# Re-ordering the start-up of a fused linear-attention and token/channel-mixer kernel on one core

## The chip, the cores and the metric

The kernel runs on one core of a Trainium2 chip. The metric is the device time of one execution in microseconds (us). All times come from the hardware profiler or from timed runs on a chip.

## The reference

For each of 8 batches (8 heads, 576 rows, head size 64): linear attention with the feature map phi, then token mixing over the 576 rows, then channel mixing over the 512 columns, both with a residual.

```python
def phi(x):
    return np.where(x > 0, x, np.exp(x) - 1.0) + 1.0
q_p, k_p = (phi(q), phi(k))
kv = np.einsum('bhsd,bhse->bhde', k_p, v)
z = np.sum(k_p, axis=2)
num = np.einsum('bhsd,bhde->bhse', q_p, kv)
den = np.einsum('bhsd,bhd->bhs', q_p, z)[..., None] + 1e-06
x = num / den                                    # then heads are joined: (8, 576, 512)
# ...
h = np.maximum(x.T @ w_tok1, 0.0) @ w_tok2       # per batch, over the rows
u = x + h.T
out = u + np.maximum(u @ w_ch1, 0.0) @ w_ch2     # 512 -> 1536 -> 512
```

## The kernel before

The instructions of each engine stand in the order in which the program emits them. TensorE does every product. ScalarE does exp, relu, the casts of v and most copies out of PSUM (the banks in which TensorE leaves its products). VectorE does the rest of phi, the division and the residual adds. SyncE issues the loads of q, k, v and the output stores; GpSimd issues the weight loads. A batch passes through these helpers:

```python
def phi(nm, n, h0, nh):          # exp on ScalarE, then add, min, max on VectorE
    # ...
    nc.scalar.activation(out=e, in_=f, func=AF.Exp)
    nc.vector.tensor_scalar(out=y, in0=f, scalar1=1.0, scalar2=None, op0=ALU.add)
    nc.vector.tensor_scalar(out=e, in0=e, scalar1=1.0, scalar2=None, op0=ALU.min)
    nc.vector.tensor_tensor(out=dst[...], in0=e, in1=y, op=ALU.max)
# vcast: v to bf16 on ScalarE; kv: k^T v; qtr: transposes of q; nd: numerator and denominator,
# then den + EPS, reciprocal and multiply on VectorE; mm1, mm2: token mixing; utr: transposes of u;
# mm3: first channel product; mm4: second channel product, then:
    o = outp.tile([128, DM], FP32, name="o_sb", tag="o_sb")      # outp has 3 buffers
    nc.vector.tensor_tensor(out=o, in0=ps, in1=u[b][:, r, :], op=ALU.add)
    nc.sync.dma_start(out=..., in_=o)
```

Batch 0 is emitted in its natural order. The preparation of batch 1 is then laid between the 24 steps ("slots") of batch 0's channel mixing, 12 of mm3 and 12 of mm4; in each of the latter, four sums of output rows grow by one weight block.

```python
c_in = [load_wc1(i) for i in range(NB)]
for g in range(2):
    landed["k1", g] = load("k", 1, g, c_in[1] if g == 0 else None)
for g in range(2):
    landed["v1", g] = load("v", 1, g)
c2_in = [after(load_wc2(0), landed["k1", 1])]
# ...
warm(40)                         # dummy matmuls
prep_k(0, 0)                     # phi of k, cast of v, for the first four heads
kv(0, 0)
warm(16)
phi("q", 0, 0, 2)
phi("q", 0, 2, 2)
qtr(0, 0)
prep_k(0, 1)
# ...
kv(0, 1)
for h0 in (4, 6):
    phi("q", 0, h0, 2)
qtr(0, 1, split=True)
# ... nd, mm1, mm2, utr, the first part of mm3
for nm in "kvq":
    for g in range(2):
        load(nm, 2, g, c2_in[2] if nm == "k" and g == 0 else None)   # batch 2, behind w_ch2
# ...
at0 = {"kv0": 13, "kv1": 15, "qt0": 19, "qt1": 21, "nd00": 22, "nd01": 22, "nd10": 22,
       "nd11": 22, "nd20": 23, "nd21": 23, "mm1": 23, "mm2a": 23, "mm2b": 23, "mm2t": 23,
       "ut": 23, "utt": 23}
fill += [(s, lambda g=g: prep_k(1, g)) for g, s in ((0, 11), (1, 12))]
fill += [(s, lambda g=g: prep_q(1, g)) for g, s in ((0, 17), (1, 19))]
```

## Time and profile before

| | before |
|---|---|
| median of the first 3 runs (range) | 317.94 us (315.82 to 318.87) |
| profiled span, granted clock of TensorE | 313.3 us, 0.953 |
| first matmuls of nd (numerator and denominator) | 16.60 us |
| second part of batch 0's channel matmuls | 42.51 us |
| batch 1's mm1 (first token matmuls) | 76.26 us |
| batch 1's channel matmuls | 86.47 us |

The profiled execution took 315.84 us, which is near the kernel's fastest.

The head of the page gives each engine's busy time, its share of the span and its instructions:

```profile
span 313.3 us, 4856 instructions
...
PE 276.7 (88%) x1882; PEld 153.6 (49%) x1882; DVE 168.4 (54%) x331; ACT 167.9 (54%) x257; POOL 10.6 (3%) x20
```

TensorE (PE) works 277 us, so nearly all that can be won is the 37 us in which it stands still. How to read the other views: a slice row gives one digit for each fortieth of the span, in tenths busy. A timeline line reads start, length, engine, line of the program, operation, output<-inputs, shape, count, and in square brackets how long the engine had been idle before it and what released it. A matmul is called hot or cold by whether its run of like matmuls takes the shorter or the longer of the two times that the traces show for it. A window line reads start:end, length, then busy time and count of PE, PEld, DVE, ACT and POOL, the granted clock, the mean busy share of the DMA engines, and GB/s.

### The profile page before, as it was taken

How to read it: one execution, taken by the hardware profiler on the slowest of the kernel's cores; microseconds unless marked ns; L12 is line 12 of the kernel's file. 1: busy time of each engine (PE TensorE's matmuls, PEld its weight loads, DVE VectorE, ACT ScalarE, POOL GpSimd, SP SyncE). 2: the span in 40 equal slices, each digit the busy share in tenths (PEclk: the TensorE clock that was granted, in tenths of full speed). 3: DMA queues.
4: the chain of work that ended last, by engine and by line, in shares of the span. 5: the costliest groups of instructions: out<-in, count | busy, mean ns of one | idle time of the engine just before them, and what ended most of it. 6: DMA issues, size and time to landing. Idle time of an engine off the chain costs nothing.

```text
span 313.3 us, 4856 instructions
## 1 busy us (share of the span) xinstructions
PE 276.7 (88%) x1882; PEld 153.6 (49%) x1882; DVE 168.4 (54%) x331; ACT 167.9 (54%) x257; POOL 10.6 (3%) x20
## 2 busy tenths in 40 slices
PE   4646689873798998999999999999999999999994
PEld 4534333441345544655566546545656455454641
DVE  6554340665447479487737760879276816250021
ACT  2552247830289835874688726765877447225600
POOL 2330300000000000000000000000000000000000
PEclk9575999996999999999999999999999999999998
DMA  7999999604979349509721972001000130011022
GB/s 209 275 168 267 280 188 271 186 0 159 294 195 304 109 150 280 174 4 273 246 69 48 273 234 70 0 33 69 35 2 1 69 100 2 18 49 70 0 67 100
DMA packets 47958, 41.82 MB, mean 133 GB/s; under 512 B 14656, under 2 KB 43200, under 8 KB 47936
## 3 DMA queue, kind: packets, MB, share of 16 engines
q1 hardware_dynamic: 43648, 37.76, 41.5%
q0 software_dynamic: 4288, 3.77, 7.7%
q8 instruction: 14, 0.23, 0.3%
q14 instruction: 8, 0.07, 0.1%
HBM read 35.85 MB, written 9.44 MB: 145 GB/s over the span
## 4 chain that ended last, share of the span: by engine, by line
PE 74%; DVE 9%; ACT 8%; DMA 4%; issue 3%; SPq 0%; ACTq 0%; DVEq 0%
PE h_ps L274 26%; PE c_ps L251 24%; PE a_ps L195 6%; PE h_ps L209 4%; ACT e L117 4%; PE kv_ps L138 3%; PE tp L152 3%; PE nd_ps L170 3%; PE c_ps L262 3%; PE tp L227 2%; DVE x L178 2%; DVE u L216 2%; DMA q_raw<-in_q_dram 2%; DMA k_raw<-in_k_dram 1%; DVE o_sb L280 1%
## 5 line engine op out<-in xcount | busy, mean ns | idle before, releaser
L251 PE MATMUL c_ps<-uT,wc 128*128 128x512 bf16 x384 | 92.6, 379 | 3.5 <-ACT cr L255 1.5
L274 PE MATMUL h_ps<-wc,cr 128*128 128x512 bf16 x384 | 90.0, 379 | 0.0
L255 ACT ACTIVATE cr<-c_ps 128x512 bf16<-128x512 f32 x96 | 56.9, 598 | 51.3 <-PE c_ps L251 51.1
L274 PEld LDWEIGHTS <-cr 128*128 128x128 bf16 x384 | 36.7, 98 | 40.6 <-issue 0.3
L251 PEld LDWEIGHTS <-wc 128*128 128x128 bf16 x384 | 35.4, 98 | 36.6 <-issue 4.3
L119 DVE TENSOR_SCALAR e<-e 128x1280 bf16<-128x1280 bf16 (+1 forms) x34 | 16.0, 471 | 39.6 <-ACT e L117 39.6
L280 DVE TENSOR_TENSOR o_sb<-h_ps,u 128x512 f32<-128x512 f32 x32 | 21.8, 685 | 22.3 <-PE h_ps L274 20.0
L178 DVE TENSOR_TENSOR x<-nd_ps,den 128x512 bf16<-128x512 f32 (+1 forms) x48 | 28.9, 602 | 1.7
L175 DVE TENSOR_SCALAR den<-nd_ps 128x8 f32<-128x8 f32 (+1 forms) x48 | 7.7, 161 | 36.5 <-PE nd_ps L170 36.0
L216 DVE TENSOR_TENSOR u<-h_ps,x 128x1024 bf16<-128x1024 f32 (+1 forms) x18 | 19.2, 1098 | 11.4 <-PE h_ps L209 11.4
L170 PE MATMUL nd_ps<-kvbd,qT 128*128 128x130 bf16 x160 | 18.3, 230 | 6.2 <-DVE x L178 4.1
L195 PE MATMUL a_ps<-x,w 128*128 128x512 bf16 (+1 forms) x72 | 19.0, 394 | 5.2 <-DVE den L175 5.2
L231 ACT COPY uT<-tp 128x1024 bf16<-128x1024 bf16 x8 | 8.1, 1012 | 28.5 <-PE tp L227 28.5
L198 ACT ACTIVATE ar<-a_ps 128x512 bf16<-128x512 f32 (+1 forms) x18 | 8.9, 545 | 27.0 <-PE a_ps L195 27.0
L170 PEld LDWEIGHTS <-qT 128*128 128x128 bf16 x160 | 12.7, 102 | 17.7 <-DVE x L178 6.0
L161 ACT COPY qT<-tp 128x1280 bf16<-128x1280 bf16 x15 | 18.5, 1231 | 4.5 <-PE tp L152 4.5
L117 ACT ACTIVATE e<-k_raw 128x1280 bf16<-128x1280 f32 x16 | 20.3, 1269 | 0.1
L117 ACT ACTIVATE e<-q_raw 128x1280 bf16<-128x1280 f32 (+1 forms) x18 | 20.2, 1148 | 0.1
L138 PE MATMUL kv_ps<-vs,kp 128*128 128x130 bf16 x160 | 12.8, 231 | 6.9 <-DVE kp L120 5.9
L209 PE MATMUL h_ps<-ar,w 128*128 128x512 bf16 (+1 forms) x72 | 16.8, 355 | 1.9 <-ACT ar L198 1.5
L128 ACT CAST vs<-v_raw 128x1024 bf16<-128x1024 f32 x16 | 16.9, 1054 | 0.0
L152 PE MATMUL tp<-identity,qp 128*128 128x128 bf16 x160 | 13.0, 230 | 4.0 <-DVE qp L120 4.0
(54 smaller groups left out, 245.3 us busy)
## 6 DMA issues: line engine op xcount, KB each, us to landing
k_raw<-in_k_dram SPq DMA_DIRECT2D x16, 512.0 KB, 5.1
v_raw<-in_v_dram SPq DMA_DIRECT2D x16, 512.0 KB, 6.2
q_raw<-in_q_dram SPq DMA_DIRECT2D x16, 512.0 KB, 6.0
out_dram<-o_sb SPq DMA_DIRECT2D x32, 256.0 KB, 2.4
wc<-in_moe_w_ch_dram POOLq DMA_DIRECT2D x8, 384.0 KB, 9.8
k_raw<-in_k_dram SPq DMA_DIRECT2D x16, 64.0 KB, 5.0
v_raw<-in_v_dram SPq DMA_DIRECT2D x16, 64.0 KB, 5.9
q_raw<-in_q_dram SPq DMA_DIRECT2D x16, 64.0 KB, 5.8
```

What stands on the lines that cost most here:

```text
L117: nc.scalar.activation(out=e, in_=f, func=AF.Exp)
L138: nc.tensor.matmul(out=ps[:, i, 0:2 * D1], lhsT=kp[b][:, r, 2 * j:2 * j + 2, :], rhs=vs[b][:, r, 2 * j:2 * j + 2, :], start=(r == 0), stop ...
L152: nc.tensor.transpose(out=tp[:, i * R1 + r, :], in_=qp[b][:, r, 2 * j:2 * j + 2, :].rearrange("p a b -> p (a b)"), identity=identity)
L170: nc.tensor.matmul(out=ps[:, i, a * 2 * D1:(a + 1) * 2 * D1], lhsT=qT[b][:, j, r, :], rhs=kvbd[b][:, j, :], start=True, stop=True)
L178: nc.vector.tensor_tensor(out=x[b][:, rs[0]:rs[0] + m, HG * D * g:HG * D * (g + 1)].rearrange("p r (h d) -> p r h d", h=HG), in0=v_[:, :, ...
L195: nc.tensor.matmul(out=ps[:, mt], lhsT=w1t[:, b, ms] if r == R else w1[:, r, ms], rhs=x[b][:, r, cs], start=(r == 0), stop=(r == R))
L209: nc.tensor.matmul(out=ps[:, i], lhsT=w2t[:, kt, b, :] if r == R else w2v[:, kt, r], rhs=ar[b][:, kt, cs], start=(kt == 0), stop=(kt == NT ...
L216: nc.vector.tensor_tensor(out=u[b][:, rs[0]:rs[0] + m, cs], in0=ps[:, 0:m], in1=x[b][:, rs[0]:rs[0] + m, cs], op=ALU.add)
L251: nc.tensor.matmul(out=ps, lhsT=wc1[:, kj, 128 * mc:128 * mc + 128], rhs=uT[b][:, kj].rearrange("p r c -> p (r c)"), start=(kj == 0), stop ...
L255: nc.scalar.activation(out=cr[b][:, mc, :], in_=ps, func=AF.Relu)
L274: nc.tensor.matmul(out=ps, lhsT=crt[:, kc, :] if t == 8 else cr[b][:, kc, 128 * r:128 * r + 128], rhs=wc2[:, kc, :], start=(kc == 0), stop ...
L280: nc.vector.tensor_tensor(out=o, in0=ps, in1=ut[p % 2] if t == 8 else u[b][:, r, :], op=ALU.add)
```

## The change

The intent is to let TensorE begin its dense work sooner, by these parts:

1. Each engine's list for batch 0 is re-ordered by when its data lands: q is loaded ahead of v; the exp table is loaded by a dummy exp during the first load; q's exps of the second half stand ahead of the copies of kv; q is transposed in pairs; the v casts go to GpSimd.
2. 130 dummy matmuls, and some smaller groups, fill the load wait, so that TensorE's clock is up when work comes.
3. Half of batch 0's residual is added by a matmul with the identity, and copied out by ScalarE, beside the other half on VectorE.
4. Batch 1's preparation moves to earlier slots.
5. w_ch2's first quarter is loaded behind batch 1's v instead of its k.
6. Its second quarter is gated on batch 1's q, where it had no gate of its own.

Smaller edits, not in the list or the cut below: w1 is gated on batch 0's q rather than its k, batch 2 is loaded in the order k, q, v, some memsets move to GpSimd, and parts of batch 0 use other PSUM banks.

```diff
-    for nm in "kvq":
+    for nm in "kqv":                       # order of batch 0's loads
+    one = work.tile([128, 1], FP32, name="one", tag="one", bufs=1)
+    nc.vector.memset(one, 0.0)
+    nc.scalar.activation(out=one, in_=one, func=AF.Exp)
 ...
-    warm(40)
-    prep_k(0, 0)
-    kv(0, 0)
+    phi("k", 0, 0, HG)
+    warm(130)
+    phi_exp("q", 0, 0, 2)
+    phi_add("q", 0, 0, HG)
+    phi_exp("q", 0, 2, 2)
+    vcast(0, 0, nc.gpsimd)
+    for j in range(2):
+        phi_end("q", 0, 2 * j, 2)
+        qtr_pair(0, j, bank16(), True)
 ...
+    phi_exp("q", 0, 4, 2)
+    phi_add("q", 0, 4, HG)
+    phi_exp("q", 0, 6, 2)
+    vcast(0, 1, nc.gpsimd)
 ...
+    kv(0, 1, True)
 ...
+    mm2_first(0, [0, 1], True)             # True: residual by an identity matmul
+    mm2_first(0, [2, 3], False)
 ...
-    c2_in = [after(load_wc2(0), landed["k1", 1])]
+    c2_in = [after(load_wc2(0), landed["v1", 0])]
 ...
-    c2_in += [load_wc2(i) for i in range(1, NB)]
+    c2_in += [after(load_wc2(i), landed["q1", 0] if i == 1 else None) for i in range(1, NB)]
 ...
-    at0 = {"kv0": 13, "kv1": 15, "qt0": 19, "qt1": 21, "nd00": 22, "nd01": 22, "nd10": 22,
-           "nd11": 22, "nd20": 23, "nd21": 23, "mm1": 23, ...
+    at0 = {"kv0": 12, "kv1": 12, "qt0": 14, "qt1": 16, "nd00": 17, "nd01": 18, "nd10": 19,
+           "nd11": 20, "nd20": 21, "nd21": 22, "mm1": 23, ...
-    fill += [(s, lambda g=g: prep_k(1, g)) for g, s in ((0, 11), (1, 12))]
-    fill += [(s, lambda g=g: prep_q(1, g)) for g, s in ((0, 17), (1, 19))]
+    fill += [(8, lambda: phi("k", 1, 0, HG)), (9, lambda: phi("k", 1, HG, HG)),
+             (11, lambda: vcast(1, 0)), (12, lambda: vcast(1, 1)),
+             (14, lambda: phi("q", 1, 0, HG)), (14, lambda: phi("q", 1, HG, HG))]
```

## The prediction

> **What bounds it now.** I read the page's forty slices first, then a table of busy time by stretch, then the timeline.
>
> ```profile
> PE   4646689873798998999999999999999999999994
> ...
> PEclk9575999996999999999999999999999999999998
> DMA  7999999604979349509721972001000130011022
> ```
>
> A slice is 7.8 us. TensorE is 90% busy or more nearly everywhere from slice 11 on; the first ten slices are not, and the granted clock dips there to half. So the kernel is bound by TensorE, behind a start-up bound by something else. The stretch table (length, busy us and count of each engine, clock, DMA) sizes both:
>
> ```profile
> 16.60:28.40 11.80, 5.18 (x42) 3.88 (x43) 6.85 (x18) 4.95 (x8) 1.95 (x3) 0.64 1.21 209
> ...
> 66.05:76.26 10.21, 2.88 (x25) 1.50 (x24) 7.17 (x20) 0.57 (x1) 0.00 (x0) 0.82 0.22 79
> 76.26:86.47 10.21, 7.93 (x41) 3.68 (x42) 4.22 (x7) 2.10 (x3) 0.00 (x0) 0.85 1.00 276
> 86.47:140.00 53.53, 50.73 (x370) 28.09 (x368) 35.19 (x72) 39.57 (x60) 0.00 (x0) 1.00 0.61 176
> 140.00:313.30 173.30, 169.24 (x1135) 91.56 (x1132) 89.83 (x166) 93.37 (x143) 0.00 (x0) 0.99 0.27 83
> ```
>
> From 86.47 us, where batch 1's first channel matmuls start, TensorE is busy for 220 of 227 us: nothing to win there, and this part only moves. Everything that the change can gain lies before it. The timeline gives three facts:
>
> ```profile
> 5.73 1.28 ACT L117 ACT_TABLE_LOAD   x1 [5.73 <-DMA k_raw<-in_k_dram]
> ...
> 10.36 0.49 DVE L118 TENSOR_SCALAR y<-q_raw 128x640 bf16<-128x640 f32 x1 [0.68 <-DMA q_raw<-in_q_dram]
> ...
> 42.51 1.46 PE L251 MATMUL c_ps<-uT,wc 128*128 128x512 bf16 x6 [0.78 <-DVE uT L233]
> ...
> 71.34 4.49 SPq L283 DMA_DIRECT2D out_dram<-o_sb  x4
> 74.77 0.69 DVE L280 TENSOR_TENSOR o_sb<-h_ps,u 128x512 f32<-128x512 f32 x1 [2.27 <-DMA out_dram<-o_sb]
> ...
> 76.26 1.89 PE L195 MATMUL a_ps<-x,w 128*128 128x512 bf16 x4 [5.20 <-DVE den L175]
> ```
>
> The table load sits between k's landing and its exp. Batch 0's dependent chain (attention, token mixing, transposes) reaches the second part of its channel matmuls only at 42.51. And the fourth output add waits on VectorE for a free buffer while batch 1's last normalisations stand behind it; TensorE idles 5.20 us and then runs cold.
>
> **What the Trainium skill says.** "ScalarE: Activation LUTs", What ACT_TABLE_LOAD costs: about 1283 ns for the load. The trace agrees: 1.28 us. "TensorE: Matmul & The Clock Gate", Part 1: an idle window of about 3.4 us halves the clock, sustained work restores it. The trace agrees in kind: after the 5.20 us gap the ten matmuls of L195 take 3.85 us, at 112.57 us the same ten take 2.17. "GPSIMD Engine Reference", Engine selection and Specifications: one-input work is roughly line-rate there, and it contends with VectorE for SBUF. The trace before has no such cast; a POOL memset of 512 elements takes 0.52 us. "DMA: Bandwidth & Descriptors", Issuing engines are not separate DMA queues: all queues share the 16 engines. The DMA row agrees: near full until slice 6 whichever queue feeds it.
>
> **Part 1, batch 0's first half.** k lands 5.6 us in. With the table already loaded, exp (1.27) ends at 7.0 rather than 8.29, min (0.49) and max (0.83) at 8.4 rather than 9.68. q is now second, and something second (v) had landed by 8.20 before; two exps of 0.68 end by 9.5, VectorE's add 0.83 and twice min and max (0.32 + 0.49) by 11.0, transposes and two copies of 0.69 by 12.2. v, now third, lands at 10.36; the POOL cast is my estimate, 1.04 us by the memset's rate plus some waiting, so 11.8. Then the kv matmuls (0.57 hot) and two copies (0.54): the nd matmuls start at 13.0 rather than 16.60. That is 3.6 us. The 130 dummies: 40 took 3.79 us before, the last ones about 50 ns each, so 130 end at 9.7 to 11, as q's first pair becomes ready; they cost nothing and keep the clock up.
>
> **Part 2, the second half.** k lands at 12.54, exp now runs 13.0 to 14.3 (16.44 to 17.71 before). VectorE does one normalisation (0.17 + 0.20 + 0.69), then k's min and max, to 15.9. q's exps no longer stand behind the kv copies on ScalarE (they were at 23.18); they end by 16.6, q is ready at 18.4 (26.09 before), qT at 19.5 (28.1 before): 8.6 us. The token matmuls then wait for weights: w1t, issued after the second cast at about 17.6 and 3.5 us to landing, is there at 21; the first half of mm1 ends at 22 (1.1), relu 0.6, and mm2 waits for w2 (issued by 18.8, 4.3 to 5.0 to landing) until 24. The residual by identity moves one of two 0.68 us adds from VectorE to a 0.6 us copy on ScalarE, at two more matmuls, so the halves run side by side: u 25.7, mm1's second half and transposes 26.9, uT 27.6, first channel matmuls (1.46) 29.1, second half of mm2 30.3, u 31.0, transposes and split copies 32. Against 42.51 that is 10.5. I take off 2 by judgement, 1.5 for the shared SBUF port and late weights and 0.5 for cold matmuls: **8.5 us**, start at 34.
>
> **Part 3, batch 1's preparation.** The rest of the channel matmuls takes 9.7 as before (42.51 to 52.20): to 43.7. From 52.20 to 76.26 were 24.06 us: 48 matmuls of h_ps (10.4), 2 kv (1.5), 2 transposes (1.5), 6 nd (2.2) make 15.6, so 8.5 idle. Afterwards the nd steps end a slot before the output adds, which removes the 5.20; their 0.2 to 0.7 us waits, 2.1 in all, spread into slots of matmuls. But the two exps now stand in slots 8 and 9, ahead of the last relus that free the four PSUM banks: 2 us; the vs casts hold up kv by about 1.2, q's chain the transposes by 1.5, others 0.8. So 5.5 idle in place of 8.5: **3 us**.
>
> **Part 4, token stage of batch 1.** mm1 runs hot, 3.85 to 2.16: 1.7. The buffer wait now falls while mm1 runs; only some 0.9 of it comes back in front of the u adds. **0.8 us** net.
>
> **Part 5, the loads.** w1 is gated on q rather than k, and POOL casts v before it issues w1t, w2, wc1: wc1's second quarter lands at some 26 rather than 24.34, and batch 1's loads, gated on it, start 2 us later. k1 then lands near 35, wanted at 39; v1 at 40, wanted at 44; q1 at 43, wanted at 48; w_ch2's quarters from 41 to 48, wanted from 43 on, a quarter each 3 to 4 us. Hidden, with 2 to 5 us to spare.
>
> Sum: 8.5 + 3 + 0.8 = 12.3, and behind it the stream of 227 us unchanged. From the median 317.94: 305.6, call it **305.5 us**.
>
> **Rivals.** First, POOL: if a cast takes 3 us rather than 1.2 (contention, or a slow first call), w1t, w2 and wc1 issue 3 or more later, and mm2 waits for w2; for it speaks that nothing in the trace sizes the cast, against it POOL's memset rate. That gives 309. Second, the transfers replace the waits: the DMA row is full until 46 us, so a shorter compute chain meets k1, v1, q1 and w_ch2 unlanded; about half of the gain is handed back, 311. Against it: before, batch 1's k had landed at 33.17 and was first used at 52.90. Third, the dummies block real work: TensorE works in order, and 130 at the mean of the first 40 (95 ns) would end at 13.7, delaying the first half by 3, the sum by perhaps 2: 307. Fourth, everything goes as worked out and no allowance is needed: 302.
>
> **Range and chances.** The losses are independent and small, the gain sits in one serial stretch that nothing later can take back, since TensorE is full behind it. I take 300 to 311. Faster by 2% means under 311.6, which the three worse rivals only just meet one at a time: 0.92 faster, 0.07 same, 0.01 slower.
>
> **What would show it.** In the trace after: the first nd matmuls at about 13 us; the second part of the channel matmuls at 32 to 36; batch 1's mm1 (ten matmuls of 512) at about 64.5 and in 2.2 us, without the 5 us gap; batch 1's channel matmuls at 74 in place of 86.47; from there to the end 227 us. I am wrong if a POOL cast lasts over 2.5 us, if TensorE waits on a wc or k_raw DMA before 60 us, or if the stretch behind grows, by a load or output store that comes at a worse time.

## The result

| | before | after |
|---|---|---|
| median (range), 4 runs each | 318.18 us (315.82 to 318.87) | 301.06 us (300.62 to 302.12) |
| ratio of the rounds (95%) | 1 | 0.9479 (0.9423 to 0.9536) |
| profiled span, granted clock | 313.3 us, 0.953 | 300.3 us, 0.988 |

A ratio is the mean time of one kernel's runs over the mean of the other's in the same rounds, so it is not quite the ratio of the medians. Executions over 1.5% slower than the fastest of the same kernel are left out of the means. The kernel is faster by 5%, at the lower end of the range given. The profiled pair shows only 13.0 us of the 17 us between the medians: the profile of before is of one of its fastest executions, and that of after is of its slowest (302.12 us). Over the 25 later runs the kernel before spread from 313.82 to 319.67 us. What causes that spread was not found.

The page of the kernel after, with the rows that answer to those of before:

```profile
span 300.3 us, 5077 instructions
...
PE 277.8 (92%) x1992; PEld 158.5 (53%) x1992; DVE 166.9 (56%) x324; ACT 167.4 (56%) x258; POOL 14.0 (5%) x24
...
PE   8968867976899989999999999999999999999994
...
PEclk9989999997999999999999999999999999999999
DMA  7969999997997595097308650011000210011022
```

TensorE's busy time has hardly moved, though 13.5 us of it are now dummies (7.8 before). A slice is 7.5 us, and from slice 10 on none but the last is below 80%. The DMA row is the one to look at: counted from slice 0, it is near full in most slices up to slice 9, 75 us, where before it broke off in slices 7 to 9. The windows of the three late stages:

```profile
42.70:61.36 18.66, 14.28 (x110) 8.10 (x109) 12.38 (x28) 10.58 (x15) 2.45 (x3) 1.00 0.98 208
61.36:72.40 11.04, 6.93 (x41) 3.76 (x40) 5.95 (x9) 2.10 (x3) 0.00 (x0) 0.94 0.83 250
72.40:300.30 227.90, 221.01 (x1502) 119.92 (x1500) 125.20 (x237) 132.89 (x202) 0.00 (x0) 0.99 0.38 113
```

The first is the stage from the last of batch 0's first channel products to batch 1's mm1. It takes 18.66 us, where it took 24.06 before, and the DMA engines are 98% busy in it (44% before). The second, batch 1's token stage, takes 11.04 us for 10.21: it is no shorter. From the timeline of the kernel after, the lines that answer to the prediction's:

```profile
0.75 1.28 ACT L391 ACT_TABLE_LOAD   x1 [0.75 <-PEq L591]
...
9.73 1.05 POOL L146 CAST vs<-v_raw 128x1024 bf16<-128x1024 f32 x1 [6.57 <-DMA v_raw<-in_v_dram]
...
13.63 0.62 PE L196 MATMUL nd_ps<-kvbd,qT 128*128 128x130 bf16 x8 [0.18 <-ACT kvbd L169]
...
32.60 1.70 PE L332 MATMUL c_ps<-uT,wc 128*128 128x512 bf16 x6 [0.67 <-ACT uT L313]
...
38.51 0.74 POOL L417 DMA_DIRECT2D wc<-in_moe_w_ch_dram  x1 [16.13 <-DMA v_raw<-in_v_dram]
...
42.56 2.59 POOL L417 DMA_DIRECT2D wc<-in_moe_w_ch_dram  x3 [3.31 <-DMA q_raw<-in_q_dram]
...
45.43 1.04 PE L355 MATMUL h_ps<-wc,cr 128*128 128x512 bf16 x4 [2.72 <-DMA wc<-in_moe_w_ch_dram]
...
60.32 0.93 SPq L105 DMA_DIRECT2D v_raw<-in_v_dram  x1
...
61.36 1.03 PE L231 MATMUL a_ps<-x,w 128*128 128x512 bf16 x4
...
62.15 6.20 SPq L364 DMA_DIRECT2D out_dram<-o_sb  x4
...
67.31 0.69 DVE L361 TENSOR_TENSOR o_sb<-h_ps,u 128x512 f32<-128x512 f32 x1 [3.98 <-DMA out_dram<-o_sb]
...
69.18 0.59 PE L242 MATMUL h_ps<-ar,w2t 128*128 128x512 bf16 x2 [2.65 <-DVE u L248]
```

The table load is out of the way, nd comes 3.0 us sooner, the second part of the channel matmuls 9.9 us sooner, and mm1 follows without the 5.20 us gap. But two waits are new. At 42.7 us TensorE stands still for 2.72 us, for w_ch2's first quarter, which was issued at 38.51. And the fourth output add waits 3.98 us on VectorE for a store: the stores were issued from 62.15 on, right behind the last load of batch 2 at 60.32 in the same queue. The residual adds of batch 1 stand behind that add, so TensorE waits 2.65 us for them.

In the profiled pair the difference therefore adds up as follows. The channel matmuls of batch 0 start 9.9 us sooner; their second part takes 10.10 us for 9.69, which costs 0.4; the stage up to mm1 gives 5.4; the token stage costs 0.8; the rest of the program takes 227.9 us for 226.8, which costs 1.1. That is 13.0 us. The split is that of one execution. In the profile of after_again, the same kernel run once more (below), the stage up to mm1 takes 20.35 us and gives only 3.7, the token stage takes 9.07 us and gives 1.1, and the rest takes 226.7; the two stages together give 4.6 us in after and 4.9 in after_again.

### The profile page after: what moved, and what is told of

The parts are those of the page before. It is cut to its first block, busy times and chain, and to the rows that moved or that the text cites. A ratio compares the mean times of both kernels' runs of the same rounds, so it can differ in the third digit from the quotient of the medians.

```text
span 300.3 us, 5077 instructions
## 1 busy us (share of the span) xinstructions
PE 277.8 (92%) x1992; PEld 158.5 (53%) x1992; DVE 166.9 (56%) x324; ACT 167.4 (56%) x258; POOL 14.0 (5%) x24
## 4 chain that ended last, share of the span: by engine, by line
PE 70%; DMA 9%; ACT 7%; SPq 5%; DVE 3%; issue 2%; POOL 1%; ACTq 0%; DVEq 0%
PE h_ps L355 28%; PE c_ps L332 23%; PE a_ps L231 4%; PE h_ps L242 4%; SPq L105 3%; PE nd_ps L196 3%; PE c_ps L343 3%; DMA wc<-in_moe_w_ch_dram 3%; DMA v_raw<-in_v_dram 2%; PE tp L175 2%; ACT e L114 2%; PE tp L259 2%; SPq L103 2%; DMA q_raw<-in_q_dram 2%; PE kv_ps L165 2%
## 5 line engine op out<-in xcount | busy, mean ns | idle before, releaser
L332 PE MATMUL c_ps<-uT,wc 128*128 128x512 bf16 x384 | 93.8, 382 | 3.2 <-ACT cr L336 1.5
L128 DVE TENSOR_SCALAR e<-e 128x1280 bf16<-128x1280 bf16 (+1 forms) x34 | 17.0, 500 | 32.9 <-ACT e L114 32.9
L187 ACT COPY qT<-tp 128x1280 bf16<-128x1280 bf16 x14 | 17.2, 1231 | 2.1 <-PE tp L175 2.1
L248 DVE TENSOR_TENSOR u<-h_ps,x 128x1024 bf16<-128x1024 f32 x14 | 16.5, 1217 | 0.7 <-PE h_ps L242 0.7
L234 ACT ACTIVATE ar<-a_ps 128x512 bf16<-128x512 f32 x14 | 7.5, 592 | 15.7 <-PE a_ps L231 15.7
L242 PE MATMUL h_ps<-ar,w 128*128 128x512 bf16 x56 | 14.4, 379 | 0.8 <-ACT ar L234 0.7
L144 ACT CAST vs<-v_raw 128x1024 bf16<-128x1024 f32 x14 | 14.8, 1058 | 0.0
L385 PE MATMUL bank<-identity 128*128 128x128 bf16 x178 | 13.5, 247 | 1.4 <-POOL identity masks.py:199 1.4
L231 PE MATMUL a_ps<-x,w 128*128 128x512 bf16 x56 | 14.4, 379 | 0.0
L120 DVE TENSOR_SCALAR y<-k_raw 128x1280 bf16<-128x1280 f32 x16 | 13.2, 822 | 2.0 <-DMA k_raw<-in_k_dram 1.7
```

Of the source, the lines that this page charges most:

```text
L187: nc.scalar.copy(out=qT[b][:, 2 * g:2 * g + 2].rearrange("p j r c -> p (j r) c"), in_=tp[:, 0:2 * R1])
L231: nc.tensor.matmul(out=ps[:, mt], lhsT=w1t[:, b, ms] if r == R else w1[:, r, ms], rhs=x[b][:, r, :], start=(r == 0), stop=(r == R))
L242: nc.tensor.matmul(out=ps[:, i], lhsT=w2t[:, kt, b, :] if r == R else w2v[:, kt, r], rhs=ar[b][:, kt, :], start=(kt == 0), stop=(kt == NT ...
L248: nc.vector.tensor_tensor(out=u[b][:, rs[0]:rs[0] + m], in0=ps[:, 0:m], in1=x[b][:, rs[0]:rs[0] + m], op=ALU.add)
L332: nc.tensor.matmul(out=ps, lhsT=wc1[:, kj, 128 * mc:128 * mc + 128], rhs=uT[b][:, kj].rearrange("p r c -> p (r c)"), start=(kj == 0), stop ...
```

## The experiments

All kernels gave correct results. Ratios are to the kernel before on the same chip. Each of the three calls had its own chip, so times are compared within a call, or by ratio across calls. The first call held after_again, slots_undone, gate_k and late_fourth, the second slots_only, no_dummies, cast_act and no_identity_add, the third the rest. The kernel after, unchanged, ran again in the first call only, so in the other two a difference from it is seen through the ratios alone. Their intervals reach about 0.5% to either side, so a difference between two of them under some 2 us can't be told:

> The changed kernel once more, as the reference on this chip for the runs beside it. Expected 301 us (300.6 to 302.1 measured), a ratio to before of 0.948.

It took 300.81 us (ratio 0.9522, 0.9474 to 0.9570), with a span of 298.6 us. Its profile shows the wait for w_ch2 again (3.17 us), and a shorter wait of the fourth add (1.96 us).

| run | median us (range) | ratio (95%) |
|---|---|---|
| slots_undone | 307.13 (306.38 to 307.57) | 0.9702 (0.9665 to 0.9740) |
| gate_k | 299.64 (298.95 to 300.31) | 0.9468 (0.9431 to 0.9505) |
| late_fourth | 300.37 (298.90 to 300.83) | 0.9483 (0.9441 to 0.9525) |
| slots_only | 309.85 (307.72 to 310.75) | 0.9790 (0.9722 to 0.9858) |
| no_dummies | 300.63 (300.06 to 301.20) | 0.9508 (0.9457 to 0.9559) |
| cast_act | 298.90 (298.56 to 300.30) | 0.9462 (0.9407 to 0.9516) |
| no_identity_add | 300.40 (299.35 to 300.95) | 0.9490 (0.9426 to 0.9555) |
| exp_q_late | 300.96 (299.99 to 301.29) | 0.9483 (0.9435 to 0.9530) |
| order_kvq | 300.68 (300.10 to 302.89) | 0.9502 (0.9443 to 0.9562) |
| wc2_first | 302.90 (301.94 to 303.68) | 0.9548 (0.9507 to 0.9588) |
| best2 | 295.00 (294.52 to 295.65) | 0.9302 (0.9265 to 0.9340) |

### The slots, undone and alone

`slots_undone` is the kernel after with the old slots of batch 1; `slots_only` is the kernel before with the new ones.

```diff
 # slots_undone, against the kernel after (slots_only is the reverse, against the kernel before)
-    at0 = {"kv0": 12, "kv1": 12, "qt0": 14, "qt1": 16, "nd00": 17, "nd01": 18, "nd10": 19, ...
+    at0 = {"kv0": 13, "kv1": 15, "qt0": 19, "qt1": 21, "nd00": 22, "nd01": 22, "nd10": 22, ...
-    fill += [(8, lambda: phi("k", 1, 0, HG)), (9, lambda: phi("k", 1, HG, HG)), ...
+    fill += [(s, lambda g=g: prep_k(1, g)) for g, s in ((0, 11), (1, 12))]
+    fill += [(s, lambda g=g: prep_q(1, g)) for g, s in ((0, 17), (1, 19))]
```

> The changed kernel with batch 1's preparation put back into the old slots. Theory: the re-ordering of batch 0 alone gives the 10 us by which the channel matmuls start earlier (42.51 to 32.60), and the new slots give the rest, so this run gives back about 5 us of the profiled 14: 306 us, with the TensorE gap ahead of batch 1's ten token matmuls back at some 5 us. Rival: the slots gain nothing once batch 0 is early, because w_ch2 and the output store set the pace there: then 301 to 302.

> The kernel before with nothing of the change but batch 1's preparation in the new slots. Undoing the slots in the changed kernel cost 6.2 us. Theory: the parts are independent, so alone they gain about 5 us: 311 (ratio 0.984), with the 5.20 us gap ahead of the ten token matmuls gone and those at 2.2 us; the first part of the gain, the start of the channel matmuls at 42.5, stays as before. Rival: the slots only pay once batch 0 is early: 316.

With the old slots back the kernel takes 6.3 us longer than the unchanged one, and the gap ahead of mm1 is back. The timeline of slots_undone:

```profile
68.32 1.89 PE L231 MATMUL a_ps<-x,w 128*128 128x512 bf16 x4 [4.64 <-DVE x L209]
```

The first four matmuls take 1.89 us, as in the kernel before, against 1.03 in the kernel after. With the new slots alone the kernel before goes from 316.73 to 309.85 us, 6.9 us between the medians and 6.6 by the ratio (its interval reaches from 1.4% to 2.8%), and the same line of slots_only has neither gap nor cold matmuls:

```profile
70.26 1.03 PE L195 MATMUL a_ps<-x,w 128*128 128x512 bf16 x4
```

Both ways the slots are worth 6 to 7 us. In slots_only the second part of batch 0's channel matmuls still starts at 41.74 us, so what remains, about 9 us (0.9790 to 0.9522 or 0.9479; slots_undone, which has all but the slots, gains 9.2 us on the kernel before), is the rest of the change as a whole, batch 0's re-ordering above all.

### Which part of batch 0 carries it

Five kernels undo one part each, against the kernel after.

```diff
 # no_dummies
     def warm(m):
+        return
 # cast_act
-    vcast(0, 0, nc.gpsimd)
+    vcast(0, 0)
-    vcast(0, 1, nc.gpsimd)
+    vcast(0, 1)
 # no_identity_add (for both column halves)
-    mm2_first(0, [0, 1], True)
+    mm2_first(0, [0, 1], False)
 # exp_q_late
-    phi_exp("q", 0, 4, 2)                  # was ahead of the casts of v
-    phi_exp("q", 0, 6, 2)
     kv(0, 1, True)
+    phi_exp("q", 0, 4, 2)
+    phi_exp("q", 0, 6, 2)
 # order_kvq
-        for nm in "kqv":
+        for nm in "kvq":
```

> The changed kernel with every dummy matmul taken away, nothing else. Theory: TensorE then runs at half clock through batch 0; the matmuls of its chain that were seen at both clocks (kv 0.73 and 1.27, five transposes 0.45 and 0.72, ten of mm1's halves 1.1 and 2.1, six channel matmuls 1.46 and about 2.6) make some 4 us more on the path: 304 to 305. Rival: landings, VectorE and ScalarE set batch 0's pace, so under 1 us: 301 to 302.

> The changed kernel with batch 0's two v casts back on ScalarE. Theory A: each cast (1.05 us) comes back into ScalarE's row of work in batch 0's chain: 1 to 2 us more, 302 to 303. Theory B: GpSimd, freed of the second cast, issues w1t, w2 and w_ch1 some 2 us earlier, all later loads move up, and TensorE's 2.7 to 3.2 us wait for w_ch2's first quarter shrinks: 1 to 2 us less, 299 to 300.

> The changed kernel with the residual of batch 0's first two row groups added on VectorE again in place of the identity matmul and the ScalarE copy. Theory: the two 0.69 us adds of a half then stand one behind the other, 0.6 us more per half, one half hidden behind the other's matmuls: 0.6 to 1.2 us more, 301.5 to 302. Rival: hidden wholly, since the wait for w_ch2 sets the start of the output sums anyway: within 0.4 us of the changed kernel.

> The changed kernel with the two exps of batch 0's second half of q put back behind the kv copies on ScalarE, where the kernel before had them. The prediction named this re-ordering as the reason for the largest part of batch 0's gain. In the changed kernel's trace those exps run at 14.8 and 16.5 us and the kv copies end at 18.7. Theory: q, its transposes and all behind start 1.5 us later, so the second part of the channel matmuls at 34 in place of 32.5, and 1 to 1.5 us more in all. Rival: the weights or the v cast set the pace there, so within 0.5 us.

> The changed kernel with batch 0 loaded in the old order k, v, q (its engines' orders as changed; w1 then starts behind the last load). Theory: q lands third, at about 10.4 rather than 7.8, in front of more work than v has (add, two exps, min, max, transposes, copies: 4.4 us against one cast of 1.05), so batch 0 ends 1.5 to 2.5 us later and the weights start about 1 us later: 302 to 304. Rival: the wait for w_ch2 (3 us in all traces of the changed kernel) takes it up: within 0.5 us.

None of the five is measurably slower than the kernel after, within the 2 us or so that the ratios can tell; costs of 1 us, as some of the theories expected, are therefore not excluded by the times alone. The table load, the transposes by pairs and the PSUM banks were not undone. The dummies were expected to be worth 3 to 4 us; without them the time is 300.63 us. TensorE then does run cold at first, as the timeline of no_dummies shows:

```profile
9.85 0.72 PE L175 MATMUL bank<-identity,qp 128*128 128x128 bf16 x5 [9.85 <-DVE qp L129]
```

These five transposes take 0.44 us in the kernel after, but there they start 1.1 us later (10.95), since the last dummies end at 11.1 us while q had been ready at 9.84. (In after_again q was ready at 10.40, and the dummies held nothing up.) What the dummies save in clock they can partly take back in time, and the second part of the channel matmuls comes at 33.64 us for 32.60 or 32.39. That one microsecond is lost on the way: the wait for w_ch2 shrinks to 1.66 us, and the first output matmuls start at 45.41 us for 45.43 or 45.66.

The same is seen in exp_q_late (channel part at 33.90 us, wait for w_ch2 2.34) and in order_kvq (33.80 us, wait 1.73). In no_identity_add the channel part is not later at all (31.59 us): the adds on VectorE were hidden. In cast_act it starts at 31.64 us, and the time is the lowest of the five. Neither start is clearly sooner than in the kernel after, for late_fourth (below), whose batch 0 is unchanged, has 31.67; and the interval of cast_act's ratio (0.9407 to 0.9516) overlaps both of the unchanged kernel. What its trace does show is that GpSimd, freed of the casts, issues w_ch1 sooner (17.65 us, for 18.77 to 19.37 in the four profiles with an unchanged batch 0), and the loads that are gated on it follow. In the profiles a batch 0 chain that comes a microsecond later is thus not later at the end (batch 1's channel matmuls start at 72.78, 71.35 and 71.44 us in no_dummies, exp_q_late and order_kvq, for 72.40 and 71.91); the shrunken waits fit the reading that it then meets w_ch2 later. Which of the joint parts carries the 9 us can't be told from undoing them singly.

### Where the start-up is bound now

Three kernels go at the two new waits.

```diff
 # gate_k
-    c2_in = [after(load_wc2(0), landed["v1", 0])]
+    c2_in = [after(load_wc2(0), landed["k1", 1])]
 # wc2_first: w_ch2's first quarter straight behind w_ch1
     c_in = [load_wc1(i) for i in range(NB)]
+    c2_in = [load_wc2(0)]
 # late_fourth: the fourth output add goes behind batch 1's token stage
-            mm4(0, t, [kc])
+            mm4(0, t, [kc], t < R - 1)
+    fill += [(23, lambda: finish(0, R - 1))]
```

> w_ch2's first quarter gated on batch 1's k again, as before, rather than on its v. The changed kernel's trace puts 2.7 us of TensorE waiting down to this transfer. Theory A: the wait is real and on the path, so some 2 us less than the changed kernel beside it (299). Theory B: the kv matmuls right behind wait for ScalarE's v casts, done at 45.9 and 47.4 in the trace, so TensorE only waits one instruction later: within 0.7 us of the changed kernel.

> The first four output adds end in three buffers; the fourth add waits on VectorE for a store to land (3.98 us in the changed kernel's trace) and the residual adds of batch 1 stand behind it. Here the fourth add is put behind those. Theory: TensorE's 2.65 us wait for u goes, and with it the half clock of the twelve matmuls behind (3.81 us, 2.6 at full clock): 3.5 to 4 us less than the changed kernel, 297. Rival: the wait only moves to the PSUM bank that the fourth sum holds or to the later loads: within 1 us.

> The changed kernel with w_ch2's first quarter issued right behind w_ch1, ahead of batch 1's loads. Gating it on k moved its issue by 2.5 us and its landing not at all (45.5), for the queues share the DMA engines. Here it must land before 40. Theory A: TensorE's 3 us wait goes, and the sum ends 2 to 3 us earlier: 298 to 299. Theory B: behind it stand the PSUM banks held until ScalarE's last relu (44.3) and the kv matmuls that need its v casts (45.7 and 47.2), so the gain is 1 us or less: 300.

In gate_k the quarter of w_ch2 is issued 2.2 us sooner than in the kernel after, and TensorE gets it no sooner. The timeline of gate_k:

```profile
36.34 0.75 POOL L417 DMA_DIRECT2D wc<-in_moe_w_ch_dram  x1 [14.23 <-DMA k_raw<-in_k_dram]
...
45.58 1.04 PE L355 MATMUL h_ps<-wc,cr 128*128 128x512 bf16 x4 [3.05 <-DMA wc<-in_moe_w_ch_dram]
```

From issue to use are now 9.2 us for 6.9: the transfer is not late because it is issued late. The DMA engines, 98% busy in this stage of the kernel after, are the likely reason. (The kernel is 1.2 us faster than the unchanged one, just more than the spread, and between what its two theories expected; the table below suggests why, with the last load of batch 2 issued 1.0 us sooner than in after_again.)

In wc2_first the quarter has landed when it is wanted, and mm1 starts at 60.92 us. The kernel is nevertheless no faster, though both theories had it at 300 us or less: 302.90 us, some 2 us above exp_q_late and order_kvq. Its ratio (0.9548, 0.9507 to 0.9588) does not set it clear of the kernel after. Its timeline shows where the time went:

```profile
68.74 0.69 DVE L361 TENSOR_TENSOR o_sb<-h_ps,u 128x512 f32<-128x512 f32 x1 [5.85 <-DMA out_dram<-o_sb]
...
70.61 1.01 PE L242 MATMUL h_ps<-ar,w2t 128*128 128x512 bf16 x2 [4.52 <-DVE u L248]
```

The loads of batch 2 now end later, the last issue at 61.46 us, and the stores, issued behind them, free their buffer later. The wait has only changed its place. In late_fourth, on the other hand, nothing of batch 1 stands behind the fourth add any more, and still only 0.4 us is won (expected: 3.5 to 4), which is within the spread: mm1 starts at 61.57 us, for 61.36 or 62.84 in the kernel after.

Laid side by side, the profiles fit two limits, found after the runs and not before them. All numbers are starts in us:

| run | last load of batch 2 issued | fourth add | mm1 of batch 1 | batch 1's channel matmuls |
|---|---|---|---|---|
| after | 60.32 | 67.31 | 61.36 | 72.40 |
| after_again | 59.51 | 66.77 | 62.84 | 71.91 |
| gate_k | 58.55 | 65.81 | 61.19 | 70.96 |
| no_dummies | 60.55 | 67.63 | 62.40 | 72.78 |
| cast_act | 57.86 | 65.34 | 60.87 | 70.49 |
| no_identity_add | 59.60 | 67.09 | 63.56 | 72.45 |
| exp_q_late | 59.05 | 66.42 | 62.66 | 71.35 |
| order_kvq | 59.17 | 66.50 | 62.56 | 71.44 |
| wc2_first | 61.46 | 68.74 | 60.92 | 74.23 |
| slots_undone | 59.65 | 66.83 | 68.32, cold | 78.92 |
| late_fourth | 57.34 | 70.42, nothing behind it | 61.57 | 70.46 |
| best2 | 59.21 | 67.23, nothing behind it | 57.20 | 65.88 |

The fourth add comes 7.0 to 7.5 us after the last load's issue in the first ten rows, although mm1 moves by 2.7 us among the first nine and by 7.5 us with slots_undone. The channel matmuls come about 5.1 us after the fourth add or about 8.8 us after mm1, whichever is later; this gives every row within 0.5 us but slots_undone, where mm1 itself waits behind the fourth add, runs cold, and is followed 10.6 us later. For `after` that is 72.4 from the add and 70.2 from mm1; for no_identity_add 72.2 and 72.4; for late_fourth and best2 only mm1 counts, 70.4 and 66.0. The two limits lie within some 2 us of each other in most rows, so lifting one alone wins little. In the kernel before the last load was issued at 54.61 us, and the fourth add, at 74.77, was 20 us behind it: the loads did not set it there. As in slots_undone, mm1 stood behind it and ran cold.

That the last load is issued 5.7 us later, in spite of the earlier start, is in part the change's own doing. The kernel before issues all of w_ch2 from 33.17 us on, and batch 2's loads begin at 46.33:

```profile
33.17 3.01 POOL L338 DMA_DIRECT2D wc<-in_moe_w_ch_dram  x4 [14.62 <-DMA k_raw<-in_k_dram]
```

In the kernel after, the gate on q (part 6 of the change) holds the last three quarters until 42.56 us, for the last 3.31 us of which GpSimd waits on q alone, and batch 2's loads begin at 51.80. No run took this gate away. Nor did any move the stores ahead of the loads or into another queue, so that their place in the queue delays them, rather than the busy DMA engines as such, fits the table but is not shown.

`best2` was made to lift both. It takes late_fourth, wc2_first and cast_act together, and takes work off ScalarE ahead of mm1: the main casts of batch 1's v go to GpSimd, and batch 1's q exps stand ahead of its kv copies.

```diff
+    for g in range(2):
+        vcast_main(1, g, nc.gpsimd)        # emitted behind w_ch2's first quarter
 ...
-             (11, lambda: vcast(1, 0)), (12, lambda: vcast(1, 1)),
-             (14, lambda: phi("q", 1, 0, HG)), (14, lambda: phi("q", 1, HG, HG))]
+             (11, lambda: vcast_tail(1, 0)), (12, lambda: vcast_tail(1, 1)),
+             (12, lambda: phi("q", 1, 0, HG)), (12, lambda: phi("q", 1, HG, HG))]
 # and the edits of late_fourth, wc2_first and cast_act
```

> What the runs point to, together: batch 0's casts on ScalarE (cast_act gained some 2 us through earlier weights), w_ch2's first quarter right behind w_ch1, batch 1's main casts on GpSimd in place of ScalarE (2.1 us less in the row of work between 40.6 and 51 us that sets the pace there), batch 1's q exps ahead of its kv copies, and the fourth output add behind the residual adds. Theory: ScalarE sets the pace of that stretch, so mm1 of batch 1 starts at 57 to 59 rather than 61.4 to 62.8, and the whole takes 295 to 297. Rival: k, v or q of batch 1 land too late once w_ch2 goes first: 299 or more.

It took 295.00 us, a ratio of 0.9302, about 2% less than the kernel after by the ratios of the two (0.9302 over 0.9479); the expectation was met. Its windows, the same three stages as above:

```profile
41.80:57.20 15.40, 14.12 (x108) 7.89 (x107) 12.32 (x28) 8.22 (x13) 2.36 (x3) 1.00 0.88 179
57.20:65.88 8.68, 6.40 (x41) 3.26 (x40) 5.58 (x8) 2.10 (x3) 0.00 (x0) 1.00 1.12 303
65.88:292.80 226.92, 219.96 (x1503) 119.61 (x1500) 125.56 (x238) 132.89 (x202) 0.00 (x0) 1.00 0.40 118
```

The first stage has 1.3 us of idle TensorE left (15.40 less 14.12), against 4.4 in the kernel after, and ScalarE's busy time in it is down from 10.58 to 8.22 us. The second is 2.4 us shorter. How much each of best2's edits gives was not separated.

## Why the prediction was right or wrong

The direction and the range held; the predicted time was 4.4 us too high. By its own steps:

- **Part 1** held in kind. nd starts at 13.63 us, 0.6 late. The GpSimd casts took 1.05 and 1.32 us where 1.2 was estimated, so that rival fell. The contention with VectorE that the prediction took from "GPSIMD Engine Reference", Specifications, is seen: beside the casts a 128x640 min on VectorE took 1.20 us and a 128x1280 add 1.57, where cast_act, without such casts, has 0.32 and 0.83. Of "they cost nothing and keep the clock up", said of the dummies, each half held only in part. In the profile of after they held the first transposes up by 1.1 us, in that of after_again by nothing. They did keep the first transposes hot (0.44 us for 0.72), but eight dummies at 20.14 us were cold again in after (1.06 us for 0.61). In the whole they were worth nothing measurable.
- **Part 2** was sized right, 9.9 us in the profile for 8.5; the allowance of 2 us taken off by judgement was too large. The reasons given inside it were borne out only in small part: q's exps put back behind the kv copies made the channel part start 1.3 to 1.5 us later, where the step names this order as the reason that q is ready 8.6 us sooner; the residual put back on VectorE made it no later; and neither changed anything measurable in total. Only the chain as a whole is shown to be worth about 9 us.
- **Part 3** named the right mechanism, the 5.20 us gap ahead of mm1, and sized it too low. The sum of Parts 3 and 4 was 3.8 us, against 4.6 and 4.9 in the two profiles of the kernel after, and slots_only and slots_undone both measured 6 to 7. The mis-sized term is the idle time: the step had it fall from 8.5 to 5.5 us, and it fell from 8.9 to 4.4 (4.9 in after_again), although 2.72 of what remained was a wait for w_ch2 that the step did not contain.
- **Part 4** held for mm1, which ran hot. Its other half did not hold in the profile of after: "only some 0.9 of it comes back" was said of the buffer wait; 2.65 us of TensorE's time came back. (In after_again, where mm1 came 1.5 us later, it was 0.63, and the stage gained 1.1 us.) Before, the stores went out 17 us after the last load of batch 2, and the add waited 2.27 us; after, they went out 2 us behind it, and it waited 3.98. The step did not ask what would stand ahead of them once the compute came sooner.
- **Part 5** fell: "Hidden, with 2 to 5 us to spare". w_ch2's first quarter was to land at 41 us; it was issued at 38.51 and came only at 45.4, and TensorE waited 2.72 us for it. That is one of the prediction's own signs of being wrong (a wait for wc before 60 us), and the second rival, transfers that take the place of the waits, was right in kind. Its 311 us was not reached, although the two new waits for transfers (2.72 and 2.65 us) are nearly the half of the gain that it wrote off, because Parts 2 and 3 gained more than was allowed them.
- **The stretch behind**, taken as unchanged at 227 us, was 227.9 (226.7 in after_again).

In the profiled pair the steps come to 13.0 us for 12.3, so under- and overestimates nearly cancelled, which is luck. Most of the remaining 4.4 us is the base: the sum was taken off the median of before, 317.94 us, while the profile behind it was of an execution of 315.84; and after's profile was of its slowest run. Those two differences, 2.1 and 1.1 us, are chance in which executions were profiled, not insight.

## What to carry to other kernels

When a start-up chain is shortened, list for each later stage which transfer must have landed by then and what stands ahead of it in its queue; the output stores of one batch behind the prefetches of the next are easily missed, and here they went with a landing time that the order of the compute hardly moved. If undoing single parts of a change moves nothing, look for two limits that lie close together, and test an edit that lifts both. Clock-warming dummies and engine offloads should be tried alone before they are kept: here each could be taken back at no measurable cost.

## What the Trainium skill lacked or had wrong

- "TensorE: Matmul & The Clock Gate", Part 1, warns that clock events of a trace can be unreliable. The runs show a case of it: in no_dummies the granted clock reads 0.999 over the whole run, while the first matmuls, until about 25 us, took far longer than the same ones later or with dummies ahead of them (five transposes 0.72 us for 0.44; four 256-column matmuls 1.06 for 0.60).
- No page has a figure for what a queue in a saturated stream adds to a transfer that stands behind others. Here stores behind a run of loads freed their buffer 7.0 to 7.5 us after the last load's issue in ten profiles, though they were issued at 61.7 to 64.4 us themselves, and a weight quarter issued 2.2 us sooner landed no sooner (6.9 and 9.2 us from issue to use).
